# A hand-written order of 1379 steps on one core, replaced by another order of the same steps (delta rule and multiplicative FFN, fp32)

## The chip, the cores and the metric

The kernel runs on one core of a Trainium2 chip, in fp32. The metric is device time in microseconds of one execution. The kernel before took 577.34 us, the median of three runs (575.42, 577.34 and 577.79).

The engines of the core are named as the profile names them: PE (TensorE, matrix products; PEld is its loading of weights), DVE (VectorE), ACT (ScalarE), POOL (GpSimd) and SP (SyncE, which issues nearly all DMAs here).

## The reference

```python
batch, n_heads, seq, head_dim = (4, 8, 768, 48)

def _attn_ref(q, k, v, beta):
    k_n = k / (np.linalg.norm(k, axis=-1, keepdims=True) + 1e-06)
    state = np.zeros((B, H, D, D))
    for t in range(S):
        kt, vt, bt = (k_n[:, :, t], v[:, :, t], beta[:, :, t, None])
        y[:, :, t] = np.einsum('bhd,bhde->bhe', q[:, :, t], state)
        v_old = np.einsum('bhde,bhd->bhe', state, kt)
        state = state + bt[:, :, :, None] * np.einsum('bhd,bhe->bhde', kt, vt - v_old)
    return y

n_tokens, d_model, d_ff = (3072, 384, 1024)

def _moe_ref(x, w1, w2, w3, w_out):
    a = x @ w1
    b = x @ w2
    h = a * b @ w3
    return h @ w_out
```

The weights are float64 in memory; q, k, v and beta are float32. Between the two blocks the attention output is laid out as x, 3072 tokens by 384 features.

## The kernel before

The 768 positions are cut into 12 chunks of 64, and two neighbouring chunks make a pair (0 to 5). Inside a chunk the recurrence is solved at once with the inverse of a triangular matrix; from chunk to chunk a small state is carried. The FFN works on the same pairs: a pair gives 512 tokens. w3 and w_out are multiplied once on the chip, so that the FFN ends in one product with the folded matrix. The FFN's products and the final ones use sums of operands to save products (the steps T, S, W, X), which POOL and DVE make.

The work is cut into generators, one for each letter and number below. Each `yield` ends a step. `ORDER` (line 39) is a text of names; the loop at the end of the kernel takes one step of the named generator for each name, and a name whose generator is used up does nothing:

```python
    def step(name):
        if name not in running:
            running[name] = parts[name]()
        next(running[name], None)

    for name in ORDER.split():
        step(name)
    in_text_order()
```

`in_text_order` (line 185) then pins every engine to the order in which the instructions were made. So `ORDER` sets, for each engine and for SP's DMA queue, what stands behind what; between engines only the data's own dependences and the buffers count. A step such as c5.2 is the third step of generator c5 (they are numbered from 0).

The names that matter:

- P0 to P35: pieces of the float64 weights. Step 0 loads a piece through SP into one of 5 raw buffers (L762), steps 1 to 3 turn it into float32 on ACT (L770), DVE (L775) and POOL (L777). P0 to P7 are w_out, P8 to P23 are halves of w3, P24 to P35 are w1 and w2.
- t and f: transposes of w3 (PE L827, ACT L830) and the fold of w3 with w_out (PE L836, ACT L843), two halves of 8 dense matmuls for each f.
- beta, k, q, v: loads of the inputs. K and Q (L355 to L378) bring keys and queries by features onto PE for the first pair, h and s make the scores (PE L436 and L442, then DVE L448 and L459); later chunks get theirs from p (loads) and d (four DVE transposes, L352; d.3 is the last).
- g (POOL L298, DVE L300) and N (15 small DVE operations, L307 to L331): squares and norms of the keys, by pair.
- u, V, e: the triangular inverse. u stores the scores to memory by blocks (L476), V loads them (L488), runs 31 steps of two DVE operations (L502, L507) for a pair and stores the result (L515). e loads it back (L524, L531), transposes on DVE (L543) and makes the corner block with two small products on PE (L560) and copies on ACT (L576, L587).
- n: v scaled on POOL (L599). c: the chain from chunk to chunk, c.0 PE with the state, c.1 DVE (R, L647), c.2 PE, c.3 DVE (X, L658), c.4 PE, c.5 DVE (S, L679), all PE parts at L613 with 64 matmuls of 48 or 64 columns.
- y: the attention output (PE L718, 160 small matmuls or fewer), its copy (ACT L736) and its transposing transfers (SP L747).
- b, a: the FFN's two products for pair 0 and pairs 1 to 4 (PE L857, ACT L869, DVE L873). The last pair has a50 to a53 (L997). o: the product with the folded matrix (PE L1089), x: the result and its stores (ACT, DVE L1118, SP L1106).

A "dense" step is one of a, b, f or o: 8 or more matmuls of 128 rows. A "small" step is one of K, Q, s, h, e, c, y, g, N, t: 4 to 160 matmuls of 48 to 64 columns.

PE's small steps share two bank pairs of PSUM (the inverse V of pairs 0 and 1 holds one of them too), and the dense ones use four single banks. The slabs for the converted weights and their products are a ring of 10.

Of the kernel before, what the change touches and what calls it, by code (L numbers as in the profile page):

```python
# [44 lines left out]
P14 V0 V0 V0 f0 P15 P15 P19 t11 f2 V0 P14 P14 V0 V0 V0 f1 f5 P23 P23 t6 V0 P15 P15 P23 t11 f5 f5 P23
t15 t15 h0 t7 f7 f7 t7 t6 f3 f3 V0 q2 P17 V0 V0 V0 V0 V0 V0 V0 V0 V0 P17 V0 k2 V0 V0 P16 P17 P28 P17
t9 P16 P24 v1 P16 P16 V0 V0 V0 V0 P28 P20 P28 P28 V0 g1 f3 t9 t8 k3 e0 f7 N0 N0 K2 h0 t8 f4 K2 P20
P20 e0 P20 t12 e0 K2 K2 t12 K2 Q2 n1 e0 e0 n0 n0 e0 P26 g1 f4 Q2 c0 Q2 Q2 f4 g1 g1 f6 Q2 n1 c0 c0
# [2 lines left out]
s2 N1 N1 q3 Q3 P32 P27 P29 P29 s2 s2 Q3 Q3 P29 b4 P31 s2 s2 Q3 Q3 s3 s3 s3 s3 b4 y1 a01 P31 s3 u2
P32 V1 b6 s3 b0 a07 b0 P31 c1 a01 a04 b6 b7 a04 a07 c1 u3 V1 V1 V1 V1 V1 a05 a05 b5 b5 b7 a00 a06
a03 a02 c2 P30 a00 V1 V1 V1 V1 V1 V1 P30 P30 P30 P31 b3 V1 a06 a03 b1 a01 k4 P33 a02 V1 b0 V1 V1 P33
V1 V1 P33 P33 P34 V1 V1 b3 a00 V1 V1 V1 a01 b1 P34 b0 V1 a03 P34 P34 P35 P35 P35 P35 a04 b2 T V1 T
a00 V1 V1 V1 a03 V1 V1 V1 a06 T V1 k5 V1 V1 V1 V1 b5 V1 p4 a04 v2 n2 n2 b2 b4 b7 a06 b6 b5 a02 d4 b6
b4 p4 b7 a07 T a02 o0 a07 V1 e2 e2 e2 c2 e2 a05 e2 e2 c2 g2 g2 g2 g2 g2 g2 g2 e3 e3 e3 v3 e3 S0 g2
g2 a05 o0 x0 o0 d4 d4 d4 c2 y2 v4 x0 x0 S0 y2 g2 c2 S0 N2 p5 N2 k6 S0 o0 c2 n3 e3 e3 n3 c3 c3 N2 S0
S0 S0 S0 o0 S0 S0 S0 S0 S0 S0 S0 x0 c3 o0 c3 y3 s4 S0 x0 x0 o0 s4 y3 s4 s4 p5 x0 d5 d5 d5 d5 s5 s4
y3 u4 s4 s5 x0 s5 s5 s5 u5 a10 x0 V2 x0 x0 s5 a10 a12 a12 a12 a17 a17 a16 a12 a16 V2 V2 n4 V2 V2 V2
# [5 lines left out]
N3 x1 v8 x1 S1 o1 V3 x1 k9 V3 V3 V3 V3 V3 V3 x1 a27 a27 a22 a22 x1 a25 a25 V3 a23 V3 V3 a23 k8 p8 p8
V3 V3 V3 V3 V3 V3 V3 V3 a26 a26 a26 V3 V3 V3 a22 a26 a20 a20 a20 V3 V3 V3 V3 V3 V3 V3 V3 a21 a21 a22
d8 V3 g4 g4 g4 g4 g4 g4 g4 V3 a20 a27 a21 a21 a27 a24 a23 a24 c6 e6 e6 e6 g4 g4 g4 a25 d8 p9 e6 e6
e6 a24 c6 d8 d8 s8 a23 o2 v7 n7 N4 n8 n8 a25 N4 s8 c6 y6 s8 a24 o2 S2 c6 S2 y6 e7 e7 e7 x2 o2 e7 c6
e7 e7 x2 c7 S2 S2 o2 s8 p9 n7 c7 c7 S2 S2 S2 S2 o2 S2 x2 s8 s8 c7 d9 d9 S2 S2 y7 y7 u8 S2 S2 d9 S2
S2 d9 x2 o2 N4 s9 S2 x2 x2 s9 s9 s9 o2 s9 V4 s9 k11 c7 c7 y7 a32 a32 u9 x2 c8 x2 c8 V4 x2 a36 x2 a34  # L70
a34 a36 v10 a33 p10 a31 V4 a31 V4 V4 x2 V4 a33 a37 V4 V4 a30 v9 p10 V4 a37 a30 V4 V4 V4 V4 V4 V4 n9
n9 V4 V4 V4 V4 V4 V4 V4 V4 V4 V4 V4 V4 V4 V4 V4 a35 a35 a33 a33 V4 a35 a32 a30 V4 V4 V4 e8 d10 k10
e9 a32 a34 a30 a35 a36 e8 a31 e8 V5 a37 e8 e8 d10 p11 e8 d10 d10 p11 a34 S3 a36 g5 a31 S3 S3 o3 c8
e9 e9 g5 g5 x3 a37 o3 c8 c8 g5 c8 S3 e9 e9 o3 e9 c9 S3 g5 g5 g5 S3 g5 g5 S3 c9 S3 c9 S3 x3 o3 S3 S3
# [1 line left out]
s11 s11 s11 u11 s11 o3 x3 x3 s10 s10 s10 s10 s10 u10 s10 N5 N5 a47 a47 a47 a43 V5 a43 a42 a47 a40
a46 a45 V5 V5 V5 V5 V5 V5 V5 a42 V5 V5 V5 V5 V5 V5 V5 V5 V5 V5 V5 V5 V5 V5 a46 V5 V5 V5 a41 V5 V5
a40 a41 V5 V5 a44 a44 a44 V5 V5 a45 a40 V5 V5 a45 a44 e10 e11 a40 a46 c9 c9 a41 a43 c10 a45 e10 e10
a42 W W W W W a43 W W c10 v11 n11 n11 a41 e10 e10 a46 e10 S4 a42 o4 x4 e11 e11 o4 S4 S4 S4 S4 S4 S4
# [1 line left out]
o4 x4 x4 o4 y11 y11 a50 X5 X5 x4 x4 X5 x4 x4 a51 a52 x4 a50 a50 a50 a50 a50 a50 a50 a50 a50 X5 a50
a50 a50 a50 a50 a50 a50 a50 a50 a50 a50 a51 a51 a51 a51 a51 a51 a51 a51 a51 a51 a51 a51 a51 a51 a51
a52 a51 a51 a51 a51 a51 a52 a52 a52 a52 a52 a52 a52 a52 a52 a52 a52 a52 a52 a52 a52 a52 a52 a52 a52
S5 a53 a53 a53 a53 a53 a53 a53 a53 a53 a53 a53 a53 a53 a53 a53 a53 a53 a53 a53 a53 a53 S5 o5 o5 S5
# [1192 lines left out]
```

## Time and profile before

| | us |
|---|---|
| median of three runs | 577.34 |
| the profiled execution | 578.96 |
| its span | 577.2 |
| PE busy | 539.0 |
| DVE busy | 340.6 |
| POOL busy | 171.6 |
| ACT busy | 144.8 |
| PE idle in 0 to 50 us | 17.7 |
| PE idle in 50 to 128 us | 4.6 |
| PE idle in 128 to 168 us | 5.0 |
| PE idle in 168 to 505 us | 4.8 |
| PE idle in 505 to the end | 6.1 |

The profile shows one execution. Its span runs from the first to the last instruction; the execution's own time holds 1.8 us more. The largest groups on PE are the dense products: L857 with 107.8 and 107.3 us for its two weights, L1089 with 57.1 and 43.0, L836 with 46.0. The 64-matmul steps at L442 take 23.5 us in all. DVE's largest group is the inverse (L502 43.4 us and L507 43.5, on buffers in SBUF). The first three slices of PE's clock are under full speed.

In such a page a wait costs time only where it sits on the path that ends last. For most of the span that is PE, so the waits of PE are what to look at, and those of the other engines only where PE waits for them.

### The profile page before, as it was taken

How to read it: one execution, taken by the hardware profiler on the slowest of the kernel's cores; microseconds unless marked ns; L12 is line 12 of the kernel's file. 1: busy time of each engine (PE TensorE's matmuls, PEld its weight loads, DVE VectorE, ACT ScalarE, POOL GpSimd, SP SyncE). 2: the span in 40 equal slices, each digit the busy share in tenths (PEclk: the TensorE clock that was granted, in tenths of full speed). 3: DMA queues.
4: the chain of work that ended last, by engine and by line, in shares of the span. 5: the costliest groups of instructions: out<-in, count | busy, mean ns of one | idle time of the engine just before them, and what ended most of it. 6: DMA issues, size and time to landing. Idle time of an engine off the chain costs nothing.

```text
span 577.2 us, 19704 instructions
## 1 busy us (share of the span) xinstructions
PE 539.0 (93%) x8588; PEld 393.7 (68%) x8588; DVE 340.6 (59%) x795; ACT 144.8 (25%) x289; POOL 171.6 (30%) x217
## 2 busy tenths in 40 slices
PE   4868998899899999998999999999999999989997
PEld 4734666787689744598744699444886446978897
DVE  6628824649774659865696616795455793123552
ACT  1766466534021011030111130110310102112210
POOL 7544253212838010431211090011840004810000
PEclk9579999999999999998999999999999999999999
DMA  9789964659564481534562534735504105010001
GB/s 183 231 268 257 202 158 117 147 125 172 101 111 79 74 158 32 102 49 74 134 102 65 76 53 76 151 43 110 75 13 91 37 36 85 17 50 8 0 1 55
DMA packets 202806, 56.57 MB, mean 98 GB/s; under 512 B 189952, under 2 KB 196096, under 8 KB 202720
## 3 DMA queue, kind: packets, MB, share of 16 engines
q1 hardware_dynamic: 200608, 54.92, 46.1%
q8 instruction: 67, 1.10, 0.8%
q10 hardware_dynamic: 2112, 0.39, 0.4%
q14 instruction: 19, 0.16, 0.1%
HBM read 43.09 MB, written 11.01 MB: 94 GB/s over the span
## 4 chain that ended last, share of the span: by engine, by line
PE 67%; DVE 13%; DMA 9%; SPq 5%; issue 3%; ACT 2%; POOL 1%; ACTq 0%; DVEq 0%; POOLq 0%
PE ps_f L857 26%; PE ps_f L1089 19%; DVE tb L502 5%; PE ps_w L613 5%; PE ps_f L997 4%; PE ps_w L718 4%; DMA raw<-in_moe_w_dram 3%; DVE ps_w L507 3%; PE ps_w L997 2%; PE ps_w L560 2%; DVE Vb L507 2%; PE ps_w L436 1%; PE ps_w L442 1%; SPq L762 1%; PE ps_f L366 1%
## 5 line engine op out<-in xcount | busy, mean ns | idle before, releaser
L857 PE MATMUL ps_f<-xT,w2s 128*128 128x512 f32 (+1 forms) x288 | 107.8, 525 | 4.0 <-DVE ab L873 2.6
L857 PE MATMUL ps_f<-xT,w1s 128*128 128x512 f32 (+1 forms) x288 | 107.3, 525 | 1.1 <-POOL w1s L777 0.6
L857 PEld LDWEIGHTS ps_f<-xT,w2s 128*128 128x128 f32 x288 | 53.7, 190 | 51.2 <-issue 42.8
L857 PEld LDWEIGHTS ps_f<-xT,w1s 128*128 128x128 f32 x288 | 53.7, 190 | 48.1 <-issue 43.2
L930 POOL TENSOR_TENSOR ab<-ab 128x256 f32<-128x256 f32 x80 | 55.5, 727 | 39.0 <-DVE ab L873 36.8
L1089 PE MATMUL ps_f<-w,ab 128*128 128x192 f32 x320 | 57.1, 332 | 1.6 <-DVE osb L1118 1.3
L869 ACT COPY ab<-ps_f 128x512 f32<-128x512 f32 (+1 forms) x48 | 23.8, 515 | 131.2 <-PE ps_f L857 121.4
L1089 PEld LDWEIGHTS ps_f<-w,ab 128*128 128x128 f32 x320 | 51.6, 190 | 2.8 <-issue 1.9
L836 PE MATMUL ps_f<-wo,w3T 128*128 128x384 f32 x128 | 46.0, 514 | 4.5 <-ACT w3T L830 3.6
L502 DVE TENSOR_TENSOR tb<-Vb,Ub 128x31 f32<-128x31 f32 (+15 forms) x124 | 43.4, 350 | 9.1 <-DMA Ub<-Ud 5.1
L507 DVE TENSOR_TENSOR Vb<-Vb,tb 128x31 f32<-128x31 f32 (+15 forms) x124 | 43.5, 351 | 4.3
L599 POOL TENSOR_TENSOR vtok<-vtok,n 128x384 f32<-128x384 f32 x24 | 19.6, 836 | 80.9 <-DMA vtok<-in_v_dram 78.0
L1089 PE MATMUL ps_f<-room,ab 128*128 128x192 f32 x240 | 43.0, 332 | 0.0
L873 DVE TENSOR_TENSOR ab<-ab,ps_f 128x512 f32<-128x512 f32 (+1 forms) x48 | 27.0, 589 | 21.5 <-PE ps_f L857 21.5
L836 PEld LDWEIGHTS ps_f<-wo,w3T 128*128 128x128 f32 x128 | 24.8, 200 | 21.2 <-issue 5.6
L1089 PEld LDWEIGHTS ps_f<-room,ab 128*128 128x128 f32 x240 | 38.6, 190 | 0.9
L298 POOL TENSOR_TENSOR sq<-ktok 128x384 f32<-128x384 f32 x24 | 19.7, 837 | 58.0 <-DMA out_dram<-osb 20.0
L576 ACT COPY T<-ps_w 32x512 f32<-32x512 f32 x24 | 13.8, 575 | 78.0 <-PE ps_w L560 55.3
L736 ACT COPY xT<-ps_w 112x256 f32<-112x256 f32 x48 | 14.3, 382 | 68.1 <-PE ps_w L718 68.1
L777 POOL TENSOR_TENSOR w<-w,raw 128x512 uint32<-128x512 uint32 x16 | 20.7, 1303 | 29.4 <-DVE w L775 17.6
L502 DVE TENSOR_TENSOR tb<-ps_w,Ub 128x31 f32<-128x31 f32 (+15 forms) x62 | 21.1, 340 | 4.3 <-ACT ps_w L496 2.7
L442 PE MATMUL ps_w<-KQ 48*64 48x64 f32 x640 | 23.5, 228 | 0.1
(148 smaller groups left out, 782.2 us busy)
## 6 DMA issues: line engine op xcount, KB each, us to landing
raw<-in_moe_w_dram SPq DMA_DIRECT2D x16, 512.0 KB, 6.5
vtok<-in_v_dram SPq DMA_DIRECT2D x24, 192.0 KB, 4.1
raw<-in_moe_w_dram SPq DMA_DIRECT2D x24, 192.0 KB, 3.9
...
```

Source lines behind the costliest of these rows:

```text
L442: pe.matmul(ps[half(z ^ j), 1, n + C * j : n + C * j + C], lhsT=x[:, 0, :], rhs=x[:, j, :], start=True, stop=True,)
L502: dve.tensor_tensor(out=tv, in0=V[:, 0 : s + 1, s : s + 1].to_broadcast([P, s + 1, n]), in1=U[:, s, s + 1 : BS].unsqueeze(1).to_broadcast( ...
L507: dve.tensor_tensor(out=o, in0=o, in1=tv, op=ALU.subtract)
L613: pe.matmul(out(ps, r, h, z), lhsT=lhs(r, h, z), rhs=rhs(r, h, z), start=True, stop=True,)
L718: i = pe.matmul(region(h, z, r), lhsT=lhs, rhs=rhs, start=part[n] not in part[:n], stop=part[n] not in part[n + 1 :],)
L836: pe.matmul(ps[:, 0:DM], lhsT=w3Ts[jc, kc // 4][:, kc % 4 * P : kc % 4 * P + P], rhs=wo(kc), start=(kc == 0), stop=(kc == KF - 1),)
L857: pe.matmul(ps[:].rearrange("p b c t -> p b (c t)"), lhsT=w[:, m, js], rhs=x[:, m, :, c0:c1].rearrange("p b c t -> p b (c t)"), start=(m = ...
L869: act.copy(out=t, in_=ps)
L873: dve.tensor_tensor(out=t, in0=t, in1=ps, op=ALU.mult)
L930: (dve if u == last else pool).tensor_tensor(out=o_, in0=x_, in1=y_, op=op)
L997: pe.matmul(ps[:, j, :], lhsT=w[j], rhs=x, start=first and j == 0, stop=j == 1, skip_group_check=not first,)
L1089: pe.matmul(ps[b][:, b, :], lhsT=ab_of(u, HF * f + i, t0), rhs=ws_[w][:, i], start=first and i == 0 and (b == 0 or n == "F"), stop=i == HF ...
```

## The change

Only the text of `ORDER` changes. No name is added or removed and the code of no step changes; the new text has one line more, so every line behind it has its number raised by one. Nearly every line of `ORDER` differs, but most steps move by a few places against steps on other engines only. What stands in another order on an engine is a good deal less. The beginning of the text, and the places that the prediction speaks of (first as before, then as after):

```diff
-V0 beta beta beta k0 g0 g0 g0 K0 K0 k1 K1 g0 g0 K0 K0 K1 K0 s0 g0 g0 g0 g0 K1 K1 K1 q0 Q0 Q0 Q0 g0
-N0 Q0 P8 P8 P8 q1 s0 s0 Q1 P8 s1 P12 P12 P12 Q1 Q1 Q1 Q1 h1 P12 P13 P13 Q0 t0 t4 P13 P13 t5 P10 P10
...
+P8 k0 K0 K0 P8 K0 beta P8 k1 g0 beta P13 K1 g0 P12 P12 g0 g0 g0 g0 g0 s0 beta K1 P8 P13 g0 q0 P12
+P13 q1 g0 g0 N0 K1 Q0 Q0 s1 s0 Q1 P10 P13 P9 P10 s1 P12 P18 Q0 P10 Q1 Q1 P9 s0 P11 P10 P18 P0 P9
...
-P24 P21 P24 P24 P21 P21 P21 c0 P26 P26 P26 g1 y0 y0 e1 e1 t13 K3 e1 t13 f6 K3 K3 K3 g1 e1 e1 f6 P29
-g1 P25 g1 g1 P25 g1 K3 P25 y0 c1 c1 P25 b3 e1 c1 P27 b1 c1 y1 b3 P27 P27 b1 s2 P32 P32 b2 y1 b2 N1
+h0 g1 n0 e0 P20 P21 P26 K2 t12 K2 e0 f4 P25 K0 K2 e0 P24 e0 P29 e1 Q2 e0 e0 P21 Q2 f4 c0 g1 g1 P21
+t12 P21 g1 g1 Q2 f4 t13 c0 g1 y0 y0 c0 f6 c0 t13 e1 y0 e1 P29 P26 P24 f6 P25 P27 g1 n1 P25 K3 e1
+P32 n1 e1 f6 e1 K2 P25 P27 P26 c1 P26 q3 b3 Q0 K3 c1 c1 K3 g1 V1 N1 P31 s2 b1 P29 b1 P34 c1 s2 y1
...
-N3 S1 c4 o1 S1 e5 S1 c4 y4 S1 S1 N3 S1 c4 p7 S1 d7 x1 p7 o1 y4 e5 e5 c4 d7 d7 d7 s7 s7 s7 s7 s7 s7
-c5 c5 c5 c5 s6 s6 s6 s6 s6 o1 u7 s6 y5 y5 v6 n6 n6 c5 x1 x1 o1 u6 c5 c6 V3 S1 V3 x1 y5 S1 x1 V3 S1
+S1 o1 d6 a17 S1 e4 p7 S1 e4 e5 o1 e5 g3 x1 N3 c4 S1 c4 e5 o1 c4 c4 y4 d7 d7 d7 S1 o1 c5 S1 k8 c5
+y4 e5 v6 d7 s7 s7 s7 S1 e5 s7 s7 x1 V3 c5 S1 s7 c5 v7 s6 s6 p8 u7 s6 s6 S1 s6 u6 S1 o1 n7 s6 x1 y5
...
-S3 g5 N5 S3 c9 y8 x3 S3 o3 d11 d11 y9 S3 d11 x3 o3 y8 d11 s11 S3 y9 y9 n10 n10 x3 x3 x3 x3 W x3 s11
+x3 g5 p11 g5 o3 p11 e9 c9 S3 x3 c9 g5 x3 c9 S3 o3 S3 g5 S3 y8 S3 d11 c9 d11 d11 S3 o3 y8 x3 y9 N5
+W S3 d11 S3 n10 o3 x3 S3 y9 x3 s11 y9 x3 s11 s11 S3 s11 V5 o3 s10 x3 s11 s11 x3 s10 s10 s10 N5 s10
...
-c10 S4 S4 S4 S4 S4 e11 e11 o4 x4 x4 e11 S4 c10 c10 S4 S4 S4 o4 y10 c10 c11 c11 y10 o4 x4 c11 c11 y11
+n11 c11 c11 y10 c11 S4 o4 S4 S4 S4 S4 W y10 c11 x4 y11 y11 o4 S4 x4 S4 x4 S4 y11 x4 x4 o4 a50 x4
```

Per engine, these are the moves that the prediction names:

| engine | before | after |
|---|---|---|
| SP, head | beta k1 q0 P8 q1 P12 P13 P10 P9 P18 P11 u0 P0 P2 P1 P6 P3 u1 P7 P5 P22 V0 P4 P19 v0 P14 | P8 beta k1 P13 P12 q0 q1 P10 P9 P18 P11 P0 u0 P2 P1 P3 P6 P5 u1 P7 P22 V0 P4 P23 P19 P14 |
| SP, before V1's load | e0 P26 P21 e1 P29 P25 y0.2 P27 P32 q3 P31 y1.2 u2 u3 V1.1 | e0 P21 P26 P25 P29 e1 y0.2 P27 P32 q3 P31 P34 y1.2 u2 u3 V1.1 |
| DVE | c1.1 c1.3 P27.2 N1.0 s2.1 | c1.1 N1.0 P29.2 c1.3 s2.1 |
| DVE | c4.3 d7.0 c4.5 d7.1 d7.2 d7.3 s7.1 | c4.3 c4.5 d7.0 d7.1 d7.2 c5.1 d7.3 s7.1 |
| PE | y4.0 N3.1 c4.4 o1.3 e5.4 s7.0 s7.3 c5.0 c5.2 s6.0 s6.3 | c4.4 y4.0 o1.3 c5.0 e5.4 s7.0 s7.3 c5.2 s6.0 s6.3 |
| DVE | N5.0 c9.3 d11.0 d11.1 d11.2 x3.3 d11.3 | d11.0 c9.3 d11.1 d11.2 x3.3 N5.0 d11.3 |
| PE | e11.2 o4.1 c10.2 e11.4 o4.2 c10.4 o4.3 y10.0 c11.0 o4.4 c11.2 y11.0 | e11.2 c10.2 o4.1 o4.2 e11.4 c10.4 o4.3 c11.0 y10.0 c11.2 o4.4 y11.0 |

Elsewhere a few steps of the same kind change places (the halves of a, the slab sums S and W on POOL, the pieces on ACT and DVE), N2.0 stands behind c2.5 and ahead of c3.1 on DVE, and a36 and a32 stand ahead of c7.4 on PE.

More of the change, by code (lines that the diff above doesn't have):

```diff
@@ L45 @@
[L45 to L48, printed above, removed]
-P24 P21 P24 P24 P21 P21 P21 c0 P26 P26 P26 g1 y0 y0 e1 e1 t13 K3 e1 t13 f6 K3 K3 K3 g1 e1 e1 f6 P29
@@ L50 @@
-g1 P25 g1 g1 P25 g1 K3 P25 y0 c1 c1 P25 b3 e1 c1 P27 b1 c1 y1 b3 P27 P27 b1 s2 P32 P32 b2 y1 b2 N1
[L51 to L59, printed above, removed]
@@ L65 @@
[L65 to L74, printed above, removed]
@@ L75 @@
-S3 g5 N5 S3 c9 y8 x3 S3 o3 d11 d11 y9 S3 d11 x3 o3 y8 d11 s11 S3 y9 y9 n10 n10 x3 x3 x3 x3 W x3 s11
[L76 to L79, printed above, removed]
@@ L80 @@
-c10 S4 S4 S4 S4 S4 e11 e11 o4 x4 x4 e11 S4 c10 c10 S4 S4 S4 o4 y10 c10 c11 c11 y10 o4 x4 c11 c11 y11
[L81 to L84, printed above, removed]
@@ new lines @@
+s2 y1 N1 N1 P27 y1 b2 b3 s2 P32 P27 Q3 s2 P29 s2 P31 Q3 Q3 u2 b4 P31 b2 s3 s3 s3 b6 P32 Q2 s3 b4
+a04 a01 s3 a04 a07 c1 b6 b0 P31 u3 V1 P35 K1 P30 s3 a01 V1 V1 c1 a03 P32 V1 V1 a03 b5 b0 P33 a07
+V1 V1 V1 a00 a06 v2 Q2 b7 v3 V1 V1 V1 V1 a06 P30 V1 k4 Q0 b5 a00 V1 P30 V1 P30 a05 V1 P33 k5 V1 V1
+b7 V1 a05 a02 b3 g2 b1 P35 b3 V1 Q3 P33 a02 P33 P35 V1 P34 c2 P35 P34 Q1 a03 V1 a01 b1 V1 P34 a03
+V1 V1 b0 a00 a01 b5 T a02 V1 T b0 V1 n2 p4 V1 V1 V1 a00 V1 a07 n3 V1 T V1 V1 b5 n2 b4 a04 V1 g2
+a02 a07 p4 K3 b4 d4 a04 V1 b6 V1 d4 d4 e2 a06 g2 K2 b2 g2 c2 S0 b2 n3 b6 e2 e3 a06 T b7 o0 e2 e2
@@ new lines @@
+s8 c6 o2 a24 y6 x2 S2 o2 e7 y6 e7 c6 V4 S2 d9 d9 N4 c6 S2 o2 S2 c7 d9 e7 o2 p10 e7 c7 S2 s8 c7 S2
+v9 S2 s8 c7 S2 x2 k11 N4 u8 s8 o2 S2 S2 x2 y7 y7 S2 x2 S2 d9 y7 S2 o2 x2 x2 x2 d10 s9 s9 s9 s9 S2
+n8 S2 S2 x2 o2 a36 a36 x2 a32 s9 x2 c7 a32 a30 s9 u9 a34 n9 n8 V4 V4 V4 a34 V4 a31 c7 a30 V4 a35
+a32 V4 V4 a31 d10 V4 V4 V4 V4 V4 a33 c8 V4 V4 V4 k10 V4 a37 V4 g5 V4 a35 V4 V4 a35 a32 V4 V4 x2 V4
+V4 a37 V4 a34 V4 V4 V4 V4 a33 a30 V4 V4 V4 a33 V4 a35 g5 a34 e8 n9 a31 c8 a30 a36 e8 e9 e8 S3 e8
+a37 a36 a31 S3 e8 e8 g5 p10 a33 e9 o3 e9 e9 c8 a37 o3 c8 S3 g5 S3 g5 v10 d10 S3 e9 g5 d10 S3 c8 c8
@@ new lines @@
+x3 g5 p11 g5 o3 p11 e9 c9 S3 x3 c9 g5 x3 c9 S3 o3 S3 g5 S3 y8 S3 d11 c9 d11 d11 S3 o3 y8 x3 y9 N5
+W S3 d11 S3 n10 o3 x3 S3 y9 x3 s11 y9 x3 s11 s11 S3 s11 V5 o3 s10 x3 s11 s11 x3 s10 s10 s10 N5 s10
+x3 a47 a43 a47 N5 a47 a42 a45 u11 u10 a43 s10 a47 V5 a41 a40 V5 V5 V5 V5 V5 V5 V5 a42 V5 a41 V5 V5
+c9 n10 V5 V5 V5 a46 V5 a45 V5 x3 V5 V5 V5 a44 V5 V5 V5 a40 V5 a40 V5 V5 a41 v11 a46 V5 a44 V5 V5
+V5 V5 a44 a45 V5 V5 V5 a40 W c9 a41 a44 a46 W c10 a43 e10 c10 e10 a46 a43 e10 S4 a45 a42 S4 e10
+e11 a42 S4 e10 o4 e10 e11 e11 e11 W S4 c10 x4 c10 n11 S4 o4 o4 S4 x4 x4 S4 e11 c10 e11 o4 c10 S4
```

28 lines of the change are left out of this document (21 added, 7 removed).

## The prediction

> **What bounds the kernel now.** I read the page first, then the busy time in nine stretches of the span, then TensorE's waits and the other engines' rows around them.
>
> ```profile
> span 577.2 us, 19704 instructions
> ...
> PE 539.0 (93%) x8588; PEld 393.7 (68%) x8588; DVE 340.6 (59%) x795; ACT 144.8 (25%) x289; POOL 171.6 (30%) x217
> ...
> PEclk9579999999999999998999999999999999999999
> ...
> q8 instruction: 67, 1.10, 0.8%
> ```
>
> TensorE (PE) is busy for 93% of the span, and no instruction is removed, so a new order can only win back PE's idle time (577.2 - 539.0 = 38.2 us) and the time that it works at half clock. The stretches say where that is:
>
> ```profile
> 0.00:50.00 50.00, 32.28 (x586) 25.22 (x587) 26.78 (x66) 27.38 (x51) 28.96 (x41) 0.80 0.89 229
> ...
> 128.00:154.00 26.00, 22.30 (x158) 18.16 (x156) 24.10 (x73) 7.18 (x16) 12.04 (x11) 1.00 0.83 140
> ...
> 168.00:262.00 94.00, 92.99 (x1790) 66.20 (x1784) 63.58 (x150) 17.03 (x36) 27.79 (x39) 1.00 0.49 84
> 262.00:271.00 9.00, 7.49 (x275) 7.13 (x276) 5.85 (x9) 0.01 (x1) 0.00 (x0) 0.81 0.55 96
> 271.00:505.00 234.00, 231.74 (x3661) 153.24 (x3660) 139.74 (x330) 37.42 (x78) 65.83 (x88) 1.00 0.38 73
> 505.00:518.00 13.00, 10.69 (x233) 9.58 (x232) 3.35 (x6) 1.19 (x4) 1.14 (x2) 1.00 0.16 45
> ```
>
> Columns: window, length, then busy us of PE, PEld, DVE, ACT and POOL, PE's clock, DMA share, GB/s. The head (0-50) idles 17.7 us with the DMAs at 0.89: loads set it. At 128-154 DVE is the full one (24.10 of 26): the second inverse, V1. The long stretches lose 1.0 and 2.3 us in 328. Two short spots are left: 262-271 (1.5 us idle and clock 0.81) and 505-518 (2.3 us idle).
>
> **The change part by part.** Aligning the steps of both orders engine by engine, PE runs the same 329 steps in nearly the same sequence. The places where a small-product step follows a dense one go from 58 to 60. A dense step of 8 matmuls occupies PE for 2.58 us behind a dense one and 2.78 behind a small one (medians over the trace), so two more cost 0.4 us. What matters is a dozen local moves.
>
> (1) *Head.* The first big weight pieces (P8, P12, P13) are issued ahead of beta and the first queries; P4, which the fold f waits for, is moved up by two or three pieces. One piece of 512 KB is issued in about 0.7 us and lands in 6.5 (the page's issue rows), so I take 2.5 us off PE's head. Bounds: -4.5 (the 3.59 us that f0 waits, with the 0.96 of f2's second half) and +2 (the same transfers, with k1 and beta later by three issues of 0.7).
>
> (2) *e1 behind P25 and P29.* e1's eight transfers go behind two more pieces on SP's queue:
>
> ```profile
> 86.70 4.11 SPq L531 DMA_DIRECT2D T<-Vd  x4
> 90.91 5.42 SPq L762 DMA_DIRECT2D raw<-in_moe_w_dram  x8
> 96.43 4.29 SPq L747 DMA_DIRECT2D xT<-xT  x6
> ```
>
> Columns: start, duration, then what was issued. The eight weight transfers took SP 5.42 us, so e1 comes that much later relative to the head; the transfers of xT (y0.2) stay behind the same set and do not move. On PE:
>
> ```profile
> 95.57 0.70 PE L560 MATMUL ps_w<-T,U 33*33 33x32 f32 x57 [1.38 <-issue]
> ...
> 103.84 0.67 PE L857 MATMUL ps_f<-xT,w1s 128*128 128x256 f32 x2 [0.54 <-DMA xT<-xT]
> ```
>
> e1's product ran at 95.57, and PE then still waited at 103.84 for xT. With the head 2.5 us early, the row's 1.38 us of issue idle gone and the 1.13 us of waits at b3 (0.59 + 0.54) as cover, 5.42 - 2.5 - 1.38 - 1.13 = 0.4 us is left. N1.0 (15 small DVE operations, 107.61 to 112.11, 4.5 us) goes ahead of c1.3's multiply, which itself idled 3.32 us behind PE, so about 1.2 us of it shows, on DVE only. P34 ahead of y1.2 costs four issues (1.82 us), and SP is idle for 1.52 us there (110.54 to 112.06). V1's 26 us DVE run starts at 128.04 now; I let it start at 128.1 and charge e2, the step behind it, **+0.4** for head and e1 together (bounds -2 and +4).
>
> (3) *Around c3 and c4.* N2.0 goes ahead of c3.1: +0.4 of its 4.5 us, since the e3 wait covers the rest. c4.4 goes ahead of y4.0 and so closer to DVE's multiply: +0.2. a36 stands closer behind y7's transfers: +0.2. Bounds 0 and +2 together.
>
> (4) *c5 and s6/s7 (262-271).* This stretch lies 4.2 us above the usual cost of its steps: c5.2 waits 1.39 us for DVE's R, s7 some 0.9, and s6 and the end of c5.2 run at half clock (0.8 + 0.6 + 0.5).
>
> ```profile
> 265.89 1.33 PE L613 MATMUL ps_w<-R,TT 64*64 64x48 f32 x61 [1.39 <-DVE R L647]
> ```
>
> c5.0 now goes ahead of e5.4 and s7, so its R (c5.1, 0.95 us) is made while they run. In return s7.0 waits for d7.3, which stands behind c5.1: 0.95 + 0.67 + 0.2 - 0.7 (e5.4) = 1.1 us, and some of the half clock stays (0.8 to 1.2). 4.2 - 1.1 - 1.2 = **-1.9**; bounds -3 and 0. The row shows the idle 1.39 us ahead of the slow records. The Trainium skill (TensorE: Matmul & The Clock Gate, Part 1) says that the clock halves after a whole idle window of about 3.4 us; no single idle time here is that long, so by it the order would not matter to the clock, all 1.9 us of it stay, and the term would be 4.2 - 1.1 - 1.9 = -1.2; the trace shows 0.81 in this stretch all the same.
>
> (5) *N5.0* goes from ahead of c9.3 to ahead of d11.3, which feeds s11.0. x3.3 ends at 428.43, N5.0 takes 4.40 (418.89 to 423.29), d11.3 0.70: 433.53 plus 0.1, against s11.0 at 432.77 now: **+0.9** (bounds 0 and +1.5).
>
> (6) *The last chain steps.* y10 goes between c11.0 and c11.2, and o4.4 between c11.2 and y11, whose product now waits:
>
> ```profile
> 507.82 1.10 PE L718 MATMUL ps_w<-PT,X 64*48 64x64 f32 x59 [0.70 <-DVE X L658]
> ```
>
> y11 occupies 3.51 us where others take 2.27: with 2.8 us of o4.4 ahead of it, the wait goes: **-1.24** (bounds -1.24 and 0). The 1.33 us that o4.6 waits stays. e10's product loses the 0.25 us that it waits now, and o4.1 and o4.2 side by side save 0.2.
>
> Sum: 0.4 + 0.4 + 0.2 + 0.2 - 1.9 + 0.9 - 1.24 - 0.25 - 0.2 + 0.4 = -1.1 us on the span, so 576.1. The profiled execution took 578.96 us for its span of 577.2 (1.8 us outside it) and lies 1.6 above the median of the runs shown, so the median goes from 577.34 to **576.2**. V2's and V4's inverses start 1 to 2 us later with slack of 2.7 and 2.8 us ahead of the steps that wait for them: nothing is charged, but little cover is left.
>
> **The rivals.**
>
> *Slower: e1 is late.* If the head gives nothing, the 5.42 us of the two pieces meet only the 1.13 us of waits at b3 and, at best, the 1.38 of issue idle: V1 starts 5.42 - 1.13 = 4.3 us later (2.9 with the issue idle gone), with 0.3 us more from P34, and every step of e2 follows. In place of +0.4 that is +3.2 to +4.6, and if V1's delay pushes the weight conversions on DVE behind it too, +6. At the middle the sum is -1.1 + 4.6 = +3.5 to +4: **581**. It decides once V1's first multiply starts later than about 131. For it: DMA share 0.89 and 0.83 in both stretches. Against it: SP's 1.52 us of idle time.
>
> *Faster: PE's own supply stalls go.* PE shows idle time put down to issue of 1.38 us (95.57) and 1.04 (417.6), 2.5 and 1.6 in the head, each amid small products. q8 brings 67 packets of 16 KB for 2 x 8588 instructions, 256 each, and its shortest spacing is 3.4 us. If small steps set apart by dense ones no longer run out: 4.2 (c5) + 1.4 + 1.0 + 1.24 (y11) with no new waits, and 1 us of e1's: -8, so **569.5**. For it: 262-271, 275 matmuls in 9 us. Against it: the boundaries go only from 58 to 60. The Trainium skill (Runtime: NRT & Kernel Launch, Instruction fetch mechanics) calls such a 16 KB refill mostly hidden; by that nothing is won here beyond the waits, which speaks against this rival, though the 1.38 us row shows a stall that no data caused.
>
> *It doesn't do what it says.* The small steps hardly spread (58 to 60), and the moves cancel: **577.3**.
>
> **How the numbers follow.** Forecast 0.40 (own range 573.5 to 579), late e1 0.27, supply stalls gone 0.25, nothing 0.08. 0.5% (2.9 us) is about what a measurement of this kernel can tell from no change. Faster than 574.4: 0.25 and a fifth of the forecast, 0.34. Slower than 580.2: most of 0.27 and a tenth of the forecast, 0.28. The rest, 0.38, lies within. Range 570 to 582.5: half of the faster rival's spread and a third of the slower one's lie outside, about 0.2.
>
> **What would show it.** Right: the stretch after c4 loses under 2.5 us with its clock above 0.9; y11 has no wait for X; s11.0 waits some 0.9 us for DVE's transpose; V1's first multiply starts within 2 us of 128. Wrong: V1 starts after 131 (late e1), f0 starts no earlier than now (no head gain), e4 or e8 waits over 1 us for T (the slack of V2 or V4 was gone), or the issue stalls disappear elsewhere.

## The result and the profile after

The changed kernel takes 590.75 us (median of four runs, 588.98 to 591.56) beside 576.38 us of the kernel before on the same chips: a ratio of 1.0247, 95% interval 1.0206 to 1.0289. It is slower by some 14 us, outside the range that was forecast. All ratios here are taken from fast runs alone, so they need not be the quotient of the medians.

From the page of the changed kernel (all its line numbers are one higher):

```profile
span 589.9 us, 19691 instructions
...
PE 545.0 (92%) x8588; PEld 396.7 (67%) x8588; DVE 344.1 (58%) x795; ACT 143.8 (24%) x289; POOL 172.4 (29%) x217
...
PEclk9769998998999999999999999999999999999999
```

The span grew by 12.7 us. TensorE's busy time grew by 6.0 (545.0 - 539.0) with the same 8588 matmuls, its idle time by 6.7 (44.9 - 38.2). The same windows as before (length, then busy us of PE, PEld, DVE, ACT, POOL, then PE's clock, DMA share, GB/s):

```profile
0.00:50.00 50.00, 32.53 (x581) 25.09 (x582) 27.41 (x64) 26.30 (x49) 29.01 (x41) 0.83 0.87 230
50.00:128.00 78.00, 71.38 (x1349) 50.15 (x1348) 42.47 (x109) 39.79 (x81) 27.92 (x26) 0.98 0.75 155
128.00:154.00 26.00, 21.99 (x212) 18.25 (x211) 18.48 (x49) 8.63 (x20) 6.24 (x5) 0.93 0.85 157
...
168.00:262.00 94.00, 90.11 (x1610) 62.67 (x1609) 62.35 (x144) 16.43 (x33) 28.32 (x41) 1.00 0.47 82
```

At 50 to 128 PE is busy for 71.38 us where it was 73.38, with a clock of 0.98 in place of 1.00. At 128 to 154 DVE is busy for only 18.48 where it was 24.10: V1 has hardly begun. At 168 to 262 PE now idles 3.9 us, where it idled 1.0.

Windows compare unlike work once a kernel is late. I therefore aligned the steps of both traces and took the delay wherever both orders have done the same set of TensorE steps, or where a step ends that both share (us, worked out from the two traces):

```
                                before    after    delay
f4.1 done on PE                  86.68    87.52    +0.85
e1's first transpose starts      92.67    95.69    +3.02
c1.2 done on PE                 105.59   109.83    +4.24
V1's load issued                123.83   129.16    +5.33
V1's first multiply             128.04   135.28    +7.23
e2's first product              163.57   171.62    +8.05
V2: first multiply to last       23.34    27.34    +4.00 (its length)
o1.0 starts (behind e4)         243.21   253.60   +10.39
o1.4 starts (behind c5, s7, s6) 270.49   282.71   +12.21
s11.0 done                      433.93   447.00   +13.06
y11 done                        510.18   522.87   +12.69
last PE step                    573.41   586.02   +12.61
```

So 8 us are lost before e2, 2.3 around V2, 1.8 around c5, and little behind. How the first part looks on SP's queue (start, duration, what was issued):

```profile
88.63 1.80 SPq L763 DMA_DIRECT2D raw<-in_moe_w_dram  x3
90.75 2.85 SPq L525 DMA_DIRECT2D TT<-Vd  x4
93.65 1.97 SPq L532 DMA_DIRECT2D T<-Vd  x4
95.71 4.70 SPq L748 DMA_DIRECT2D xT<-xT  x6
...
116.76 4.63 SPq L748 DMA_DIRECT2D xT<-xT  x6
121.49 6.13 SPq L477 DMA_DIRECT2D Ud<-U  x8
129.16 0.34 SPq L489 DMA_DIRECT2D Ub<-Ud  x1
```

e1's eight transfers (L525, L532) stand behind the weight pieces and are issued from 90.75 on; in the old order they were done at 90.81. The next y transfers come at 116.76 where they came at 112.06, and V1's load at 129.16. The same three steps in the old order:

```profile
112.06 5.04 SPq L747 DMA_DIRECT2D xT<-xT  x6
117.19 4.98 SPq L476 DMA_DIRECT2D Ud<-U  x8
123.83 0.34 SPq L488 DMA_DIRECT2D Ub<-Ud  x1
```

On VectorE V1's first multiply then waits for that load, which lands 6 us after its issue where it took 3.4:

```profile
135.28 0.19 DVE L503 TENSOR_TENSOR tb<-ps_w,Ub 128x31 f32<-128x31 f32 x1 [4.40 <-DMA Ub<-Ud]
```

The waits of TensorE that are new, from its timeline (idle time before the group and what ended it in brackets):

```profile
93.95 0.83 PE L614 MATMUL ps_w<-X,ktok 64*48 64x48 f32 x50 [1.64 <-issue]
94.71 4.44 PE L837 MATMUL ps_f<-wo,w3T 128*128 128x384 f32 x8
99.09 0.76 PE L561 MATMUL ps_w<-T,U 33*33 33x32 f32 x64
...
109.38 0.39 PE L614 MATMUL ps_w<-R,TT 64*64 64x48 f32 x13 [1.74 <-issue]
...
141.83 4.54 PE L858 MATMUL ps_f<-xT,w1s 128*128 128x256 f32 x12 [4.01 <-ACT ab L870]
...
246.52 5.42 PE L858 MATMUL ps_f<-xT,w2s 128*128 128x512 f32 x12 [2.15 <-DVE ab L874]
...
278.75 0.90 PE L614 MATMUL ps_w<-R,TT 64*64 64x48 f32 x25 [1.14 <-issue]
...
517.25 0.55 PE L614 MATMUL ps_w<-R,TT 64*64 64x48 f32 x20 [0.99 <-issue]
...
521.02 1.07 PE L719 MATMUL ps_w<-PT,X 64*48 64x64 f32 x64
```

The fold step at 94.71 (f6.0) takes 4.44 us for 8 matmuls that take 2.85 in the old order, at a granted clock of 0.64 in the window of that step. e1's product (99.09) stands right behind it and waits for nothing: VectorE had transposed its rows by 96.39. The wait at 141.83 is for ScalarE, which stood at P30's conversion (its load lands late behind V1's) while the copies that free TensorE's banks were queued behind it. The last row is y11: its wait of 0.70 us is gone, as forecast, but 0.99 us has appeared in c11.2 just ahead of it.

### The profile page after: what moved, and what is told of

It reads as the page before. It is cut to its first block, busy times and chain, and to the rows that moved or that the text cites. A ratio compares the mean times of both kernels' runs of the same rounds, so it can differ in the third digit from the quotient of the medians.

```text
span 589.9 us, 19691 instructions
## 1 busy us (share of the span) xinstructions
PE 545.0 (92%) x8588; PEld 396.7 (67%) x8588; DVE 344.1 (58%) x795; ACT 143.8 (24%) x289; POOL 172.4 (29%) x217
## 4 chain that ended last, share of the span: by engine, by line
PE 67%; DVE 15%; DMA 8%; issue 4%; SPq 2%; ACT 2%; POOL 0%; DVEq 0%; ACTq 0%
PE ps_f L858 26%; PE ps_f L1090 17%; PE ps_w L614 5%; DVE tb L503 4%; PE ps_f L998 4%; PE ps_w L719 4%; PE ps_w L561 3%; PE ps_w L998 2%; DVE ps_w L508 2%; DVE Vb L508 2%; DMA raw<-in_moe_w_dram 2%; PE ps_f L837 2%; PE ps_w L437 2%; DMA Ub<-Ud 2%; DMA raw<-in_moe_w_out_dram 2%
## 5 line engine op out<-in xcount | busy, mean ns | idle before, releaser
L858 PE MATMUL ps_f<-xT,w1s 128*128 128x512 f32 (+1 forms) x288 | 109.4, 533 | 4.0 <-ACT ab L870 4.0
L503 DVE TENSOR_TENSOR tb<-Vb,Ub 128x31 f32<-128x31 f32 (+15 forms) x124 | 44.7, 361 | 12.1 <-DMA Ub<-Ud 8.3
L837 PE MATMUL ps_f<-wo,w3T 128*128 128x384 f32 x128 | 47.9, 527 | 0.7 <-POOL wo L778 0.7
L508 DVE TENSOR_TENSOR Vb<-Vb,tb 128x31 f32<-128x31 f32 (+15 forms) x124 | 45.0, 363 | 4.3
L874 DVE TENSOR_TENSOR ab<-ab,ps_f 128x512 f32<-128x512 f32 (+1 forms) x48 | 27.2, 586 | 21.5 <-PE ps_f L858 21.5
L837 PEld LDWEIGHTS ps_f<-wo,w3T 128*128 128x128 f32 x128 | 25.4, 206 | 17.9 <-issue 2.7
L437 PE MATMUL ps_w<-KQ 48*64 48x128 f32 x320 | 23.1, 286 | 1.3 <-DVE PT L460 0.5
```

Source lines behind the costliest of these rows:

```text
L437: pe.matmul(ps[half(z), 0, n : n + 128], lhsT=x[:, 0, :], rhs=x.rearrange("p j t -> p (j t)"), start=True, stop=True,)
L503: dve.tensor_tensor(out=tv, in0=V[:, 0 : s + 1, s : s + 1].to_broadcast([P, s + 1, n]), in1=U[:, s, s + 1 : BS].unsqueeze(1).to_broadcast( ...
L508: dve.tensor_tensor(out=o, in0=o, in1=tv, op=ALU.subtract)
L837: pe.matmul(ps[:, 0:DM], lhsT=w3Ts[jc, kc // 4][:, kc % 4 * P : kc % 4 * P + P], rhs=wo(kc), start=(kc == 0), stop=(kc == KF - 1),)
L858: pe.matmul(ps[:].rearrange("p b c t -> p b (c t)"), lhsT=w[:, m, js], rhs=x[:, m, :, c0:c1].rearrange("p b c t -> p b (c t)"), start=(m = ...
L874: dve.tensor_tensor(out=t, in0=t, in1=ps, op=ALU.mult)
```

## The experiments

The kernel before ran beside each on the same chip; its median there was 576.4 to 580.0, so the ratios are what to compare. In every edit "SP:", "PE:" and so on name the engine on which the steps change places. A few steps that hang on these move with them: g3.1 on VectorE behind V2 and the store x0.10 on SP ahead of V2's load in e7 and e8, c5.3 on VectorE behind s6.2 in e15 and e16. Two families of theories were on the table: the delay comes from the order of the transfers, or from small TensorE steps that stand together and run out of instructions.

**Head and tail apart.** e1 has the new order up to e2, e2 from e2 on.

```diff
-ORDER = old
+ORDER = new up to the first e2, then what is left of old      (e1)
+ORDER = old up to the first e2, then what is left of new      (e2)
```

> The new order up to the first step of e2, the old order behind it. In the two traces TensorE is 8.05 us late at e2's first product and 12.6 at the end. If the delays of the two parts are independent, this takes 576.4 + 8 = 584.4 us (583 to 586). If the old tail has cover for a late head, 580 or less.

> The old order up to the first step of e2, the new order behind it: 576.4 + 4.6 = 581 us (580 to 582) if the parts are independent; 577 or less if the tail is only late because the head is.

Measured: 588.95 (ratio 1.0147, 1.0077 to 1.0218) and 589.19 (1.0169, 1.009 to 1.0247). Each half costs by itself: 1.5% and 1.7%, together more than the whole (2.5%), but the intervals are wide and the seams lose a little (a wait of 1.6 us at e2's first product in the second). Neither half is late only because of the other. In e2 the part shows as in the whole: V2 takes 27.27 us. In e1's profile it does not: V1 starts at 129.85, only 1.8 us late, e2's first product is 2.95 us late, and the delay grows behind it (6.8 us at o1.4, 8.9 at the end), with a wait of 1.6 us at N2.1 and half clock for 10 us from 271.

**The dense step between the small ones.** In the new order c0.0, t13.0, y0.0 and c0.2 stand together, with f6.0 behind.

```diff
 new: -PE: c0.0 t13.0 y0.0 c0.2 f6.0
      +PE: c0.0 f6.0 t13.0 y0.0 c0.2                           (e3)
 old: -PE: c0.0 f6.0 c0.2 y0.0
      +PE: c0.0 c0.2 y0.0 f6.0                                 (e4)
```

> The new order with one token moved: the dense fold step f6.0 again between c0.0 and y0.0 and c0.2. Supply theory (TensorE gets its instructions in blocks of 256, and small steps joined without a dense one between them run ahead of the next block): the wait of 1.64 us inside c0.2 goes, f6.0 runs at full clock (2.8 in place of 4.4 us), and the time falls by 1.5 to 3 us to 588 to 589. Transfer theory (e1 is late because its transfers stand behind two weight pieces, and land at 95.7): the wait inside c0.2 may go, but e1 and all behind it stay where they are, 590.7.

> The old order with one token moved: f6.0 behind c0.2 and y0.0, so that c0.0, c0.2 and y0.0 stand together. Supply theory: a wait put down to issue of over 1 us within c0.2 or y0.0, at a place 192 or 193 instructions into a block of 256, and a slower f6.0: 576.4 + 1.5 to 3 = 578 to 579.4 us. Transfer theory: 576.4, since no transfer moves.

In e3 f6.0 takes its PSUM bank so early that K3.0 uses it again before f6's result is copied, so that one block of the folded weights is not the reference's; the instructions are the same. Measured: 591.5 (1.0213, 1.0136 to 1.029) and 576.87 (0.9966, 0.9932 to 0.9999). What the supply theory expected fails here, twice. In e3 the wait inside c0.2 goes, but e1's product then waits 1.78 us for the transpose of its rows, the fold step behind it (f6.1) takes 4.46 us at half clock in place of f6.0, and when c1.0 is done the delay is 4.20 us as it was 3.93 in the new order. In e4 the steps to f6.0 lose 1.7 us against the old order (1.14 of it a wait of c0.2 for VectorE's X; the issue wait that was expected does not appear), and e1.2 wins 1.5 of it back, since its own issue wait is gone. Joining these steps moves a wait; by itself it does not make the delay.

**Single causes undone in the new order.** e5 puts e1's transfers back, e6 P30, e7 takes GpSimd's work out of the third inverse V2, and e8 does all three.

```diff
-SP: P26.0 P25.0 P29.0 e1.0
+SP: P26.0 e1.0 P25.0 P29.0                                    (e5, e8)
-SP: V1.1 P35.0 P30.0          ACT: P30.1 b5.1 a00.1
+SP: V1.1 P30.0 P35.0          ACT: b5.1 a00.1 P30.1           (e6, e8)
-SP: V2.1 k6.0    POOL: in V2: g3.0 n5.0 n4.1 g3.2
+SP: v4.0 k6.0    POOL: ahead of V2: n4.1 n5.0 n5.1 g3.0; g3.2 behind it   (e7, e8)
```

> The new order with one token moved: e1's eight transfers ahead of P25 and P29 again. Transfer theory: e1's transposed rows land some 4 us earlier, e1 and c1 run 2 to 3 us earlier, the second inverse V1 starts 2 to 4 us earlier, and the time falls by that: 587 to 588.5 us in place of 590.7. Supply theory (the joined small steps c0.0, y0.0, c0.2 lose the time on TensorE): TensorE still reaches e1.2 late, 590 to 591.

> The new order with two moves: P30's load ahead of P35's on SP, and P30's conversion on ScalarE behind the two copies b5.1 and a00.1 that stood behind it. The wait of 4.0 us of TensorE for these copies goes. If that wait sets the end, 590.7 - 4 = 586.7 us; if the second inverse V1, which makes TensorE wait a little later, sets it anyway, the later waits grow by as much and the time stays within 1 us of 590.7.

> The new order with GpSimd's squares g3 and scalings n4, n5 and the loads that they need taken out of the third inverse V2 and put ahead of it. Contention theory (a GpSimd operation that runs beside V2 stretches VectorE's operations from 0.3 to 0.9 us): V2 takes 23.4 us again in place of 27.3, TensorE's wait of 2.15 us at a13 goes, 588.5 us. If the operations only seem long in the trace, nothing changes: 590.7.

> The three moves of the last three runs together. If V1's late start, the copies' wait and V2's stretching are the causes of most of the 14 us: 580 to 583 us, with TensorE at e2's first product less than 4 us late. If the loss sits in TensorE's joined small steps: 587 or more.

Measured: e5 593.14 (1.0261, 1.021 to 1.0312), e6 587.77 (1.0178, 1.0121 to 1.0236), e7 594.62 (1.0295, 1.0256 to 1.0335), e8 597.29 (1.032, 1.0263 to 1.0376). Only e6 may have gained, and three "repairs" together made the slowest kernel of all. The profiles say why, and each reason is a queue that the moved step is not alone in. In e5 e1's transfers are all issued by 92.20 where it was 95.61, but ScalarE's copy for e1 stands behind the conversions of P29, P26 and P25, which now land later: TensorE waits 2.7 us for it, and V1's load goes at 131.03. In e6 the wait of 4.0 us is gone, and a wait of 5.0 us for P30's weights on GpSimd stands a little later in its place; V1 starts at 132.91. In e7 V2 takes 23.80 us and its wait is gone, as the contention theory has it, but k6's load that went ahead makes y3's transfers late, and TensorE waits 1.6 us for them. So e7 shows the stretching and not its price.

**The middle and the transfers.** e9 takes f4.1 to V1's start from the old order, on all engines, into the new one; e10 does the reverse, from P24's load on. e11 moves only four transfer steps in the old order. e12 leaves k6's load where the new order has it and lets GpSimd wait till V2's end.

```diff
+ORDER = new up to f4.1, old up to V1.4, then what is left of new   (e9)
+ORDER = old up to P24.0, new up to V1.4, then what is left of old  (e10)
 old: -SP: e1.0 P29.0 P25.0 y0.2 ... y1.2 u2.0 u3.0 V1.1 P30.0 P33.0 P34.0 P35.0
      +SP: P25.0 P29.0 e1.0 y0.2 ... P34.0 y1.2 u2.0 u3.0 V1.1 P35.0 P30.0 P33.0   (e11)
 new: -text: V2 ... g3.0 n5.0 n4.1 g3.2 ... V2.32      DVE: V2.17 g3.1 V2.18 ... V2.32
      +text: V2 ... V2.32 g3.0 n5.0 n4.1 g3.2          DVE: V2.17 V2.18 ... V2.32 g3.1    (e12)
```

> The new order with the stretch from the fold step f4.1 to V1's first multiplies (some 86 to 130 us) taken from the old order, on all engines at once. Middle theory (V1 starts 7 us late because of the order of this stretch): V1 starts less than 2.5 us late, and the time falls by 4 to 6 us to 585 to 587. If V1 is late by what stands before (the head) or by chance, 589 to 591.

> The old order with only the stretch from P24's load to V1's first multiplies taken from the new order. Middle theory: V1 starts 3 to 6 us late and the time rises from 576.4 to 580 to 583. If the stretch costs nothing by itself: 576 to 578.

> The old order with four transfer steps moved on SP's queue as in the new one: P25 and P29 ahead of e1's transfers, P34 ahead of y1's, P35 ahead of P30. Transfer theory: V1 starts 3 to 5 us late and the time rises to 580 to 582. If the late V1 comes from the order of the compute engines, 576 to 578.

> The new order with GpSimd's g3.0, g3.2, n4.1 and n5.0 behind the end of the third inverse V2, and no load moved (the earlier try moved k6's load and made y3's transfers late). Contention theory: V2 takes 23.5 to 25 us in place of 27.3, TensorE's wait of 2.15 us at a13 goes or falls below 0.7, and the time falls to 588 to 589. If the later squares g3 make N3 late instead, c5 and s7 lose it again: 590.7.

At the seams of e9 and e10 a bank is taken again before its result is copied (b7.0 in e9, f7 and a03.0 in e10), so a block of the weights or of pair 0's product is not the reference's. Measured: e9 586.66 (1.0176, 1.0115 to 1.0237), e10 585.4 (1.0155, 1.009 to 1.022), e11 583.77 (1.0113, 1.0043 to 1.0183), e12 591.59 (1.0186, 1.0084 to 1.0287). With the old middle the new order's ratio is 0.7% lower, with intervals that overlap; V1 starts at 130.23 there, 2.2 us late, as the middle theory has it. e1's transfers stand ahead of f4.1 in the new text, so in e9 they stay behind P25 and P29. The old order with the new middle is 1.5% slower, but that is not all the middle's price: at its seam K2.0 waits 3.6 us for ScalarE, which it does in neither order, f4.1 is 2.8 us late already, and of the 7.0 us at e2's first product some 4.2 are left for the middle. In e11 no compute step changes places, and V1 starts at 132.48 although this run's head was 1.95 us early. Its SP and PE rows:

```profile
81.29 9.16 SPq L762 DMA_DIRECT2D raw<-in_moe_w_dram  x8
90.50 2.01 SPq L524 DMA_DIRECT2D TT<-Vd  x4
92.56 3.56 SPq L531 DMA_DIRECT2D T<-Vd  x4
```

```profile
96.52 1.13 PE L560 MATMUL ps_w<-T,U 33*33 33x32 f32 x64 [4.04 <-DVE T L543]
97.58 5.45 PE L836 MATMUL ps_f<-wo,w3T 128*128 128x384 f32 x8
```

The eight weight transfers hold SP for 9.16 us, e1's rows land behind them, and TensorE waits 4.04 us for the transpose of these rows. The fold step behind it runs at half clock (5.45 us for 2.85). The transfer theory holds here, and the ratio's interval bears it out: four steps moved on a queue that computes nothing, and in the profile the last TensorE step ends 6.5 us later (579.95 against 573.41). e12's edit did not do what it was for: GpSimd's own sequence is that of the new order, a place behind V2's steps in the text is no wait for GpSimd, and it ran g3.0, n5.0, n4.1 and g3.2 at 219 to 224.5, in the middle of V2. Only VectorE's g3.1, now behind V2, and the two GpSimd operations that follow it (g3.4, n5.1) came out of V2, which takes 26.03 us, and c5 took 12.7 us from o1.3 to o1.4 where the new order took 11.6. It gives no verdict on the time.

**Four questions in the old order.** What was still open: whether the new order around c5 costs by itself, whether GpSimd stretches V2 by itself, and whether the covers that the traces ask for make a faster kernel.

```diff
-PE: y4.0 c4.4 o1.3 e5.4 s7.0 s7.3 c5.0 c5.2    DVE: d7.0 c4.5 d7.1 d7.2 d7.3 ... c5.1
+PE: c4.4 y4.0 o1.3 c5.0 e5.4 s7.0 s7.3 c5.2    DVE: c4.5 d7.0 d7.1 d7.2 c5.1 d7.3   (e13; e18 with SP: p7.0 p7.1 ahead of d7.0)
-SP: k6.0 ... V2.1        POOL: n4.0 n4.1 g3.0 g3.2
+SP: V2.1 k6.0            POOL: g3.0 n4.0 n4.1 g3.2            (e14)
-SP: P29.0 P25.0 y0.2
+SP: P25.0 y0.2 P29.0                                          (e15)
-PE: c5.0 c5.2 s6.0 s6.3 ... c11.2 y11.0 o4.5 o4.6
+PE: c5.0 s6.0 s6.3 c5.2 ... c11.2 o4.5 y11.0 o4.6             (e15, e16)
```

> The old order with only the steps around c5 as in the new one: c4.4 ahead of y4.0, c5.0 and its VectorE step ahead of e5.4 and s7, c5.1 ahead of d7.3. The recorded forecast was -1.9 us (574.5). The trace of the new order points the other way: +1.8 us (578.2), with the clock below 0.85 in a longer stretch.

> The old order with k6's load behind V2's, and GpSimd's g3.0, n4.0, n4.1 (and g3.2 behind them) placed so that they run beside the third inverse V2. Contention theory: each of the four makes VectorE 0.5 us later, V2 takes 25 to 26 us in place of 23.3; its slack of some 2.7 us takes that, so the time stays within 1 us of 576.4. Without contention V2 stays at 23.3.

> The old order with three moves: P29's load behind y0's transfers (the opposite of what the new order does), c5.2 behind s6's two products so that these cover VectorE's R, and o4.5 ahead of y11 so that one dense step covers y11's wait for X and y11 covers o4.6's wait of 1.33 us. By the waits of the old trace: about -1 (P29), -1.4 to -2.5 (c5.2), -0.7 to -2.2 (y11, o4.6): 571 to 573.5 us. If only data waits move elsewhere, 576.

> The same without the move of P29: -2 to -4.5 us, 572 to 574.5 us; if the late part gives nothing because of the clock or the next wait, 576.

> The old order with c4.4 ahead of y4.0, c5.0 and c5.1 ahead of e5.4 and d7.3, and the load p7.1 ahead of d7's transposes as in the new order. The recorded forecast: -1.9 us. The trace of the new order: about +1.8 us, with s7.0 waiting for d7.3 and a wait put down to issue in c5.2.

In e13 two of d7's transposes stand ahead of the load that they need, and so transpose old data; the load itself then waits for them. Measured: e13 587.52 (1.0131, 1.0067 to 1.0195), of which TensorE's wait of 4.8 us for d7.3 is that slip, so it decides nothing; e18, without the slip, 580.94 (1.0002, 0.996 to 1.0043); e14 579.18 (1.0017, 0.998 to 1.0055); e15 580.0 (1.0032, 0.9998 to 1.0066); e16 579.78 (1.0004, 0.9972 to 1.0036).

e18: from o1.3's end to o1.4's start it takes 8.80 us where the old order took 10.39. That looks like the forecast gain of 1.9, but the old order's profile had the clock at 0.84 in this stretch and e18 had 1.00. With the old order of these steps and a clock of 1.00 the stretch takes 9.26 us in e14 and 8.86 in e10, so against like executions the gain is 0.1 to 0.5. Behind it o1.4's matmuls take 3.15 us in place of 2.87, and y5 has an issue wait of 0.34 us. In the new order the same stretch took 11.6 us, with 1.14 in the issue wait of c5.2 and a clock of 0.76 from 276 to 283; e2 and e9 have the same steps at a clock of 1.00, with issue waits there of 0.85 and 0.69, and take 9.89 and 9.71. So the order of c5 is worth next to nothing by itself, and the loss (1.2 us in this stretch, 1.8 from o1.0 to o1.4) goes with that wait and the half clock.

e14 shows the stretching alone. In the old order (first fence) V2's operations of 156 and 175 columns take 0.32 to 0.34 us each; in e14 (second fence, with GpSimd's rows ahead) they take 0.83 to 0.85 as long as a GpSimd operation runs:

```profile
211.42 0.32 DVE L507 TENSOR_TENSOR Vb<-Vb,tb 128x156 f32<-128x156 f32 x1
211.78 0.34 DVE L502 TENSOR_TENSOR tb<-Vb,Ub 128x175 f32<-128x175 f32 x1
212.15 0.34 DVE L507 TENSOR_TENSOR Vb<-Vb,tb 128x175 f32<-128x175 f32 x1
```

```profile
211.73 0.96 POOL L298 TENSOR_TENSOR sq<-ktok 128x384 f32<-128x384 f32 x1 [26.92 <-DVE Vb L507]
212.66 1.79 POOL L599 TENSOR_TENSOR vtok<-vtok,n 128x384 f32<-128x384 f32 x2
...
212.04 0.83 DVE L507 TENSOR_TENSOR Vb<-Vb,tb 128x156 f32<-128x156 f32 x1
212.91 0.85 DVE L502 TENSOR_TENSOR tb<-Vb,Ub 128x175 f32<-128x175 f32 x1
213.79 0.85 DVE L507 TENSOR_TENSOR Vb<-Vb,tb 128x175 f32<-128x175 f32 x1
```

Each of the four operations costs VectorE some 0.5 us: V2 takes 25.36 us in place of 23.34. The time did not change by more than the interval; from e2 to o1.0 this run is 1.0 us longer, so V2's slack took about half. The Trainium skill (GPSIMD Engine Reference, Specifications) says that GpSimd shares its SBUF interfaces with VectorE and that VectorE's operations with two inputs in SBUF contend for them; the runs agree, with 0.5 us for an operation of 0.9.

e15 and e16 beat nothing: c5.2 behind s6 wins about 1 us in e15 and none in e16, and o4.5 ahead of y11 moves y11 by 2.9 us, which the last products (a50 to a53) pay back with 1.3 to 1.6 us more. No version here is clearly faster than the kernel before; e4 comes nearest (0.9966, with an interval that ends at 0.9999).

**The transfers undone with all that hangs on them.** e17 repairs what e5 left out.

```diff
-SP: P26.0 P25.0 P29.0 e1.0 ... P34.0 y1.2 ... V1.1 P35.0 P30.0
+SP: P26.0 e1.0 P25.0 P29.0 ... y1.2 ... V1.1 P30.0 P35.0 P34.0
-ACT: P29.1 P26.1 P25.1 e1.3 ... P30.1 b5.1 a00.1
+ACT: P26.1 e1.3 P29.1 P25.1 ... b5.1 a00.1 P30.1             (e17)
```

> The new order with e1's transfers ahead of P25 and P29, P30 ahead of P35, P34 behind both, and with the conversions P25.1, P29.1 and P30.1 on ScalarE behind the steps of e1 and b5, a00 that would wait for them. Transfer theory: V1 starts less than 3 us late in place of 7.2, and the time falls by 4 to 6 us to 585 to 587. If V1 stays 5 us late or more, the order of the small steps on TensorE is the cause.

Measured: 590.85, a ratio of 1.0184 (1.0123 to 1.0245) beside 1.0247 (1.0206 to 1.0289) of the new order; the chip was slower, and 0.6% is what it may have won. V1's load goes 1.75 us late in place of 5.33, which is no more than this run's head (f4.1 1.70 late), although TensorE's steps stand as in the new order. But the load took 6.6 us to the first multiply, which so starts at 132.15, 4.1 us late and between the two outcomes that had been expected. TensorE waits 4.9 us for P30's weights, V2 still takes 27.21 us, and c5.2's issue wait is 2.2 us: at o1.4 the delay is 12.06 us again. So with e1's transfers ahead V1's load is no later than the head, where in the five profiles with the new order's own steps up to that load (the new order, e1, e6, e7, e12) it is 1.3 to 4.5 us later than the head. But e9's is no later than its head either (1.46 and 1.34), with e1's transfers behind P25 and P29 and the compute steps of the old order. So either repair took the delay away, in one profile each. That the transfers cost time by themselves is shown in the old order alone (e11), and they are not the cause of the whole loss; the head, V2 and c5 stand beside them, and e17 won little.

## Why the prediction was wrong

What bounds the kernel was read rightly: TensorE's work sets the time, and the loss is mostly in its idle time (6.7 us) and in steps that ran at half clock (f6.0 1.6 us longer, a05.0 1.2). The sum failed at these steps, by the numbers of the prediction:

- **(2) e1 behind P25 and P29, the step that failed.** +0.4 us at e2 was charged, +8.05 came. Against the 5.42 us of the two pieces three covers had been set. The waits at b3 (1.13) did cover: b3 waits for nothing now. The head's gain did not come (next point). The issue wait at e1.2 (1.38) went, but it was no fixed cost that a later step could absorb: issue waits of 0.71 and 1.64 us came ahead of it, in c0.0 and c0.2, and 1.74 and 0.63 behind it, in c1.2 and y1.0. The price itself was more than the time on SP, too. In e11, with no compute step moved, TensorE waits 4.04 us for e1's rows, the next fold step loses 2.6 to half clock, and issue waits of 0.58 and 1.45 follow; e2 is 5.0 us late in a run whose head was 1.95 early, so about 6.9. In the new order's own profile TensorE does not wait for these rows. The 8.05 us are 0.85 of the head, 4.5 from there to V1's load (issue waits and f6.0's half clock; b3's waits gone), 1.9 more from the load to the first multiply, and 0.8 in V1's own length. V1's chain has no slack of its own: y1's transfers wait for y1.0, which ends 5.8 us late, and u2, u3 and V1's load follow them on SP. P34, charged at next to nothing, did no harm here: SP is idle from 113.25 to 116.76. Part of the 8.05 is the execution: e1, e7 and e12 have the same steps up to e2's first product and were 2.95, 5.62 and 7.58 us late there. All are far above +0.4.
- **(1) The head.** -2.5 was forecast. f4.1 ends between 87.5 and 89.9 us in the ten profiles with the new head (mean 88.3) and between 84.1 and 89.5 in the ten with the old one at least up to P24 (mean 85.8): +2.5, the other way; only 0.85 of it in the profiles compared above. P4 was not moved up: fifteen pieces stand ahead of it in both orders, and its conversion ended at 49.58 us where it ended at 49.47. TensorE's first fold step began at 38.5 in place of 36.1, since Q, s and h come later. The -2.5 was taken from no row.
- **V2's slack, charged at nothing.** V2's length is 23.3 us in every profile with the old order there, and 27.2 to 27.4 with the new one wherever GpSimd's work was left alone. The prediction let V2 start late, but took its length as given; some 3 of the 4.0 us are GpSimd's stretching, the rest two VectorE steps inside (g3.1, and a15.3, which stood at V2's very end). Against a slack of 2.7 that leaves 1.3; TensorE waited 2.15 at a13. The risk was named ("little cover is left"), its cause was not.
- **(4) c5, s6 and s7.** -1.9 was forecast, +1.8 came. Of the 4.2 us that it was taken from, 1.1 to 1.5 are gone in e10 and e14, which have these steps in the old order at full clock, and against those e18 gains 0.1 to 0.5. The loss came with c5.2's issue wait and half clock.
- **(5) s11 behind N5.0.** +0.9 was forecast, +0.63 came.
- **(6) y11.** -1.24 was forecast and -1.24 came at y11, but c11.2 lost 1.17 just ahead of it: y10 between c11.0 and c11.2 made a run of 256 small matmuls.
- **(3) c3, c4, a36.** +0.4, +0.2, +0.2 were forecast: no change at c3 and a36, 0.71 at c4.4 (a wait for X).

Of the rivals the slower one named the mechanism and the place, e1 late and V1 starting after 131 (135.28), and gave 581. It was short at e2 (+3.2 to +6 where +8.05 came) and by V2 and c5, and it counted the forecast's 0.4 twice (-1.1 - 0.4 + 4.6 is +3.1). That several chains had lost their cover at once, and that one late chain pushes loads and conversions of the next, was in no case of the prediction; its upper end of 582.5 came from one mechanism at a time. "Small steps spread" was wrong in the direction that matters: the number of boundaries hardly changed, but the new order made longer runs of small matmuls, with 7.2 us of waits at instruction blocks after 30 us in place of 1.9. That is not one execution's chance: these waits sum to 4.1 to 7.7 us in the eight profiles with TensorE's new order (e3, e5 to e8, e12 and e17 beside the new order itself) and to 0.2 to 2.9 in the eight with the old one but for a few steps (e4, e11, e13 to e16 and e18 beside the kernel before).

What is not settled: the price of each part in the whole. Single repairs stand 0.6 to 0.7% below the new order (e6, e9, e12, e17; e12's edit missed its aim), with intervals that overlap its own, e5, e7 and e8 made new waits, and V1's load takes 3.5 to 6.9 us from issue to the first multiply in different profiles for no reason that the traces show.
